# Attention and MLP-mixer kernel: a hand-ordered pipeline over head pairs, with column-tiled value products, 128-key blocks and channel 2 in 128-token chunks over two batches

## The chip, the cores and the metric

The kernel runs on one core of one Trainium2 chip. Its time is device microseconds of one execution. Three executions before the change took 538.24, 538.77 and 540.26 us; the median is 538.77 us. A separate, profiled execution gives the views of the trace.

The engines have short names: PE is the matmul engine, PEld its weight loads, DVE the vector engine, ACT the scalar engine, POOL the engine that here issues the input DMAs, SP the one that issues the output DMAs. A matmul has a stationary operand, brought in by a weight load, and a moving one, whose columns (448 or 384, say) are named with it; results go to PSUM, which this kernel uses in banks of 512 float32 a partition, and DVE or ACT move them to the on-chip memory.

## The reference

Eight batches, 12 heads, 448 tokens, head size 64. Attention has no softmax; its output, 448 tokens by 768 channels, goes through a mixer that works first across tokens, then across channels.

```python
def _attn_ref(q, k, v):
    S = q.shape[2]
    scale = 1.0 / np.sqrt(q.shape[-1])
    scores = scale * np.matmul(q, k.transpose(0, 1, 3, 2))
    attn = np.maximum(scores, 0.0) ** 2 / S
    return np.matmul(attn, v).astype(np.float32)

def _moe_ref(x, w_tok1, w_tok2, w_ch1, w_ch2):   # x: (8, 448, 768)
    xt = x.transpose(0, 2, 1)
    h = np.maximum(xt @ w_tok1, 0.0) @ w_tok2     # 448 -> 256 -> 448
    u = x + h.transpose(0, 2, 1)
    h2 = np.maximum(u @ w_ch1, 0.0) @ w_ch2       # 768 -> 1536 -> 768
    return (u + h2).astype(np.float32)
```

## The kernel before

The work is cut by batch. `attention_pair(b, p)` does two heads, `mixer_chunks(b)` returns the mixer of one batch as a list of 32 closures (30 for the last batch), and the loop at the end (lines 364 to 383) issues the six pairs of batch b+1 between the mixer chunks of batch b, spread evenly. The first six pairs (batch 0) run alone, with the weight loads between them.

**A pair.** Six POOL DMAs (lines 114 to 118) bring q, k and v of two heads as four chunks of 112 tokens, converted to bf16. v lands in a zero-padded tile `v_zp`, so that the value of head e fills 64 of 128 columns and the other 64 are zero. Eight matmuls with the identity transpose q and k; DVE copies the result to `qkT_sb` (line 140). For each of four blocks of 112 keys, two matmuls of 448 columns give the scores of the two heads (`sc_ps`, at rows 0 to 63 and 64 to 127 of the array). Relu and square follow: in blocks 0 and 2 ACT does the relu (line 158) and DVE the square as a scalar_tensor_tensor (line 159); in blocks 1 and 3 DVE does the relu (line 168) and ACT the square (line 175). Then two value products per block, each over the whole array because of the zero padding, add into `xTp_ps`: eight matmuls of 448 columns a pair. ACT scales the sum into `xT_sb` (line 186). These value products have a lower priority (`PRI_AV`), so the scheduler places them some instructions later.

**A mixer.** `stage_b` transposes attention back to tokens (24 matmuls, ACT copies); `stage_c1` and `stage_c2` are the token MLP, and line 256 adds the residual into `uT_sb`; `stage_d` transposes that sum to tokens again (24 matmuls, ACT copies into `u_sb`); `stage_e1` is channel 1 (12 units of six matmuls, ACT relu, line 339); `stage_e2` is channel 2 by chunks of 112 tokens: for each of 12 slices one matmul of 512 columns and one of 256 (`m2_term`, lines 294 and 301); `m2_finish` adds `u_sb` on DVE (lines 314 and 317) and stores 336 KB. In the last batch, two chunks of channel 2 are taken along with channel 1.

**What sets the order.** A scheduler orders each engine by program order, priority and what it knows of readiness; an engine then runs its own list strictly in order. PSUM is two buffers of two banks for scores and `qkT_ps` (`ps_att`), one bank for `xTp_ps`, three single banks for everything of the mixer (`ps_mlp`).

Of the kernel before, what the change touches and what calls it, by code (L numbers as in the profile page):

```python
# [14 lines left out]

PRI_AV = 48
# [3 lines left out]
def kernel(  # L20
# [18 lines left out]
    SC = 4  # L39
    S_CH = S // SC  # L40
    NP = H // 2
    CC = DM // 128
    EC = DC // 128
    JC = DT // 128
    N0 = 512
    N1 = DM - N0
    NV = 3
# [5 lines left out]
    qkv = ctx.enter_context(tc.tile_pool(name="qkv", bufs=5))  # L53
    attn = ctx.enter_context(tc.tile_pool(name="attn", bufs=2))
    batch = ctx.enter_context(tc.tile_pool(name="batch", bufs=2))
# [3 lines left out]
    ps_mlp = ctx.enter_context(tc.tile_pool(name="ps_mlp", bufs=3, space=bass.MemoryType.PSUM))  # L59

    ident = consts.tile([128, 128], BF16)
    make_identity(nc, ident)

    v_tiles = []
    for i in range(NV):
        vt = consts.tile([S_CH, SC, 2, 2 * D], BF16, name=f"v_zp{i}")
        nc.gpsimd.memset(vt, 0.0)
        v_tiles.append(vt)

    wt1 = wpool.tile([S_CH, SC, DT], BF16)  # L70
    wt2 = wpool.tile([128, JC, S], BF16)
    wc1 = wpool.tile([128, CC, DC], BF16)
    wc2 = wpool.tile([128, EC, DM], BF16)

    def load_weights(step):
        if step == 0:
            nc.gpsimd.dma_start(
                out=wt1, in_=moe_w_tok1.rearrange("(c s) j -> s c j", c=SC)
            )
            nc.gpsimd.dma_start(  # L80
                out=wt2, in_=moe_w_tok2.rearrange("(c j) s -> j c s", c=JC)
            )
        elif step in (1, 2):
            for g in range(3 * (step - 1), 3 * step):
                nc.gpsimd.dma_start(
                    out=wc1[:, g, :], in_=moe_w_ch1[128 * g : 128 * (g + 1), :]
                )
        else:
            for e in range(4 * (step - 3), 4 * (step - 2)):
                nc.gpsimd.dma_start(  # L90
                    out=wc2[:, e, :], in_=moe_w_ch2[128 * e : 128 * (e + 1), :]
                )

    xT_tiles = {}

    def mm_lp(*args, pri=0, **kwargs):
        if pri:
            with tc.high_priority(offset=-pri):
                nc.tensor.matmul(*args, **kwargs)  # L99
        else:  # L100
            nc.tensor.matmul(*args, **kwargs)  # L101

    def attention_pair(b, p):
        if p == 0:
            xT_tiles[b] = batch.tile([128, NP, S], BF16, name="xT_sb")
        xT_sb = xT_tiles[b]
        h0 = 2 * p
        v_bf = v_tiles[(b * NP + p) % NV]

        q_raw = qkv.tile([S_CH, SC, 2, D], BF16, name="q_raw")  # L110
        k_raw = qkv.tile([S_CH, SC, 2, D], BF16, name="k_raw")
        for hh in range(2):
            src = q[b, h0 + hh].rearrange("(c s) d -> s c d", c=SC)
            nc.gpsimd.dma_start(out=q_raw[:, :, hh, :], in_=src)  # L114
            src = k[b, h0 + hh].rearrange("(c s) d -> s c d", c=SC)
            nc.gpsimd.dma_start(out=k_raw[:, :, hh, :], in_=src)  # L116
            src = v[b, h0 + hh].rearrange("(c s) d -> s c d", c=SC)
            nc.gpsimd.dma_start(out=v_bf[:, :, hh, hh * D : (hh + 1) * D], in_=src)  # L118

        qkT_ps = ps_att.tile([128, 2, S], BF16, tag="att", name="qkT_ps")  # L120
        for c in range(SC):
            mm_lp(
                qkT_ps[:, 0, c * S_CH : (c + 1) * S_CH],
                lhsT=q_raw[:, c],
                rhs=ident[:S_CH, :S_CH],
                is_transpose=True,
                start=(c == 0),
                stop=False,
            )
        for c in range(SC):  # L130
            mm_lp(
                qkT_ps[:, 1, c * S_CH : (c + 1) * S_CH],
                lhsT=k_raw[:, c],
                rhs=ident[:S_CH, :S_CH],
                is_transpose=True,
                start=False,
                stop=(c == SC - 1),
            )
        qkT_sb = attn.tile([128, 2, S], BF16, name="qkT_sb", bufs=3)
        nc.vector.tensor_copy(qkT_sb, qkT_ps)  # L140

        xTp_ps = ps_acc.tile([128, S], FP32, name="xTp_ps")
        for c2 in range(SC):
            sl2 = slice(c2 * S_CH, (c2 + 1) * S_CH)
            sc_ps = ps_att.tile([128, 2, 512], FP32, tag="att", name="sc_ps")
            for e in range(2):
                hsl = slice(64 * e, 64 * (e + 1))
                mm_lp(
                    sc_ps[:S_CH, e, :S],
                    lhsT=qkT_sb[hsl, 1, sl2],  # L150
                    rhs=qkT_sb[hsl, 0, :],
                    start=True,
                    stop=True,
                )
            at_sb = attn.tile([128, 2, S], BF16, name="at_sb", bufs=10)
            at2_sb = attn.tile([128, 2, S], BF16, name="at2_sb", bufs=10)
            if c2 % 2 == 0:
                nc.scalar.activation(at_sb[:S_CH], sc_ps[:S_CH, :, :S], AF.Relu)  # L158
                nc.vector.scalar_tensor_tensor(  # L159
                    out=at2_sb[:S_CH],  # L160
                    in0=at_sb[:S_CH],
                    scalar=1.0,
                    in1=at_sb[:S_CH],
                    op0=ALU.mult,
                    op1=ALU.mult,
                )
            else:
                nc.vector.tensor_scalar(  # L168
                    out=at_sb[:S_CH],
                    in0=sc_ps[:S_CH, :, :S],  # L170
                    scalar1=0.0,
                    scalar2=None,
                    op0=ALU.max,
                )
                nc.scalar.activation(at2_sb[:S_CH], at_sb[:S_CH], AF.Square)  # L175
            for e in range(2):
                mm_lp(
                    xTp_ps,
                    lhsT=v_bf[:, c2, e, :],
                    rhs=at2_sb[:S_CH, e, :],  # L180
                    start=(c2 == 0 and e == 0),
                    stop=(c2 == SC - 1 and e == 1),
                    pri=PRI_AV,
                )

        nc.scalar.activation(xT_sb[:, p, :], xTp_ps, AF.Copy, scale=float(alpha2))  # L186

    def mixer_chunks(b):
        xT_sb = xT_tiles[b]
        last = b == B - 1  # L190
        chunks = []
        state = {}

        def stage_b(c):
            if c == 0:
                state["x_sb"] = batch.tile([S_CH, SC, DM], BF16, name="x_sb")
            x_sb = state["x_sb"]
            x_ps = ps_mlp.tile([128, DM], BF16, tag="bank", name="x_ps")
# [151 lines left out]
        def stage_e2(c):  # L350
            state["m2_%d" % c] = m2_alloc(c)
            for e in range(EC):
                m2_term(c, e)
# [58 lines left out]
```

## Time and profile before

| what | value |
|---|---|
| median of three runs | 538.77 us |
| span of the profiled execution | 538.1 us |
| instructions, matmuls among them | 7873, 3104 |
| mean granted clock of PE | 0.976 |
| HBM read, written | 43.38 MB, 11.01 MB |
| input DMAs of q, k, v | 288, of 56 KB each |

The span runs from the first to the last instruction of the program; the execution's time is the span and under a microsecond around it. A busy share says how long some instruction of that engine was under way, and since matmuls overlap in the array, a PE that is 92% busy isn't a PE at its peak: how fast matmuls follow one another is read from their starts in the timeline.

### The profile page before, as it was taken

To read this page: it belongs to the slowest core of one execution; us is meant where nothing else is said; L and a number is where in the kernel's file an instruction comes from. 1 tells how busy PE (TensorE), PEld (TensorE's weight loads), DVE (VectorE), ACT (ScalarE), POOL (GpSimd) and SP (SyncE) were. 2 spreads that over 40 slices of the span, in tenths; PEclk is the share of its full clock that TensorE was granted. 3 is DMA by queue.
4 is the path that set the end of the run, shared out by engine and by line. 5 is a ranking of instruction groups with operands and counts; after the bars stand their busy time and mean duration, and the time that the engine had idled before them with its cause. 6 is when DMAs were issued, how large, how long until landed. Compare 5 with 4: busy or idle time off the path is not lost.

```text
span 538.1 us, 7873 instructions
## 1 busy us (share of the span) xinstructions
PE 493.6 (92%) x3104; PEld 274.6 (51%) x3104; DVE 286.3 (53%) x352; ACT 297.6 (55%) x433; POOL 214.9 (40%) x317
## 2 busy tenths in 40 slices
PE   1678999999899989999899989999899998999996
PEld 1223444575446644475445744466445744566554
DVE  1565675627754396626855287434856277441202
ACT  2454777707873378706874269625776078733320
POOL 9679983515534263614553244522544132000000
PEclk9986599999999999999999999999999999999999
DMA  7999994837665665735676467554847352002003
GB/s 66 163 170 153 91 79 27 51 87 67 42 39 54 102 43 36 48 64 77 43 46 59 87 45 50 34 78 70 51 32 49 85 52 18 0 27 78 0 1 102
DMA packets 141092, 33.22 MB, mean 62 GB/s; under 512 B 134464, under 2 KB 136704, under 8 KB 141056
## 3 DMA queue, kind: packets, MB, share of 16 engines
q0 software_dynamic: 136960, 21.71, 54.6%
q1 hardware_dynamic: 4096, 11.01, 6.8%
q8 instruction: 24, 0.39, 0.3%
q14 instruction: 12, 0.10, 0.1%
HBM read 43.38 MB, written 11.01 MB: 101 GB/s over the span
## 4 chain that ended last, share of the span: by engine, by line
PE 63%; ACT 18%; DMA 6%; POOL 5%; DVE 4%; issue 3%; DVEq 0%; ACTq 0%; POOLq 0%
PE m_ps L332 17%; PE m2a_ps L294 14%; PE xTp_ps L99 8%; PE m2b_ps L301 7%; PE sc_ps L101 6%; ACT at_sb L158 6%; DMA wc<-in_moe_w_ch_dram 4%; ACT u_sb L278 4%; ACT x_sb L208 3%; PE h_ps L249 3%; ACT at_sb L175 2%; PE qkT_ps L101 2%; PE t1a_ps L222 2%; DVE at_sb L159 2%; DVE at_sb L168 2%
## 5 line engine op out<-in xcount | busy, mean ns | idle before, releaser
L114 POOL DMA_DIRECT2D q_raw<-in_q_dram x96 | 67.6, 707 | 165.5 <-PE qkT_ps L101 136.0
L168 DVE TENSOR_SCALAR at_sb<-sc_ps 112x896 bf16<-112x896 f32 x96 | 104.4, 1088 | 51.5 <-PE sc_ps L101 51.4
L332 PE MATMUL m_ps<-uT_sb,wc 128*128 128x448 bf16 x576 | 125.3, 354 | 1.8 <-ACT u_sb L278 1.8
L294 PE MATMUL m2a_ps<-wc,r_sb 128*112 128x512 bf16 x360 | 115.3, 379 | 0.0
L158 ACT ACTIVATE at_sb<-sc_ps 112x896 bf16<-112x896 f32 x96 | 88.3, 919 | 40.2 <-PE sc_ps L101 40.0
L99 PE MATMUL xTp_ps<-at_sb,v_zp 112*128 112x448 bf16 x384 | 109.3, 378 | 0.2
L159 DVE SCALAR_TENSOR_TENSOR at_sb<-at_sb 112x896 bf16<-112x896 bf16 x96 | 104.1, 1086 | 6.3 <-ACT at_sb L158 5.3
L175 ACT ACTIVATE at_sb<-at_sb 112x896 bf16<-112x896 bf16 x96 | 91.5, 954 | 21.4 <-DVE at_sb L168 20.8
L118 POOL DMA_DIRECT2D v_zp<-in_v_dram x96 | 67.2, 706 | 66.3 <-PE xTp_ps L99 63.5
L301 PE MATMUL m2b_ps<-wc,r_sb 128*112 128x256 bf16 x360 | 89.6, 272 | 0.0
L332 PEld LDWEIGHTS <-wc 128*128 128x128 bf16 x576 | 52.4, 98 | 60.1 <-issue 20.7
L101 PE MATMUL sc_ps<-qkT_sb 64*112 64x448 bf16 x384 | 71.3, 399 | 5.7 <-ACT at_sb L158 2.6
L116 POOL DMA_DIRECT2D k_raw<-in_k_dram x96 | 67.7, 707 | 1.8 <-issue 0.8
L314 DVE TENSOR_TENSOR out_sb<-m2a_ps,u_sb 112x512 f32<-112x512 f32 x30 | 20.7, 692 | 89.1 <-PE m2a_ps L294 84.7
L140 DVE COPY qkT_sb<-qkT_ps 128x896 bf16<-128x896 bf16 x48 | 29.9, 622 | 70.9 <-PE qkT_ps L101 70.7
L294 PEld LDWEIGHTS <-r_sb 128*112 128x112 bf16 x384 | 49.5, 130 | 30.6 <-ACT r_sb L339 3.8
L339 ACT ACTIVATE r_sb<-m_ps 128x448 bf16<-128x448 f32 x96 | 51.3, 549 | 23.8 <-PE m_ps L332 22.8
L186 ACT ACTIVATE xT_sb<-xTp_ps 128x448 bf16<-128x448 f32 x48 | 26.5, 553 | 67.1 <-PE xTp_ps L99 57.9
L208 ACT ACTIVATE x_sb<-x_ps 112x768 bf16<-112x768 bf16 x32 | 24.2, 811 | 64.9 <-PE x_ps L200 64.8
L301 PEld LDWEIGHTS <-r_sb 128*112 128x112 bf16 x384 | 49.3, 130 | 8.1
L99 PEld LDWEIGHTS <-v_zp 112*128 112x128 bf16 x384 | 37.3, 102 | 29.7 <-issue 12.6
L101 PEld LDWEIGHTS <-qkT_sb 64*112 64x112 bf16 x384 | 25.7, 130 | 49.0 <-issue 29.0
(35 smaller groups left out, 345.2 us busy)
## 6 DMA issues: line engine op xcount, KB each, us to landing
out_dram<-out_sb SPq DMA_DIRECT2D x32, 336.0 KB, 2.7
q_raw<-in_q_dram POOLq DMA_DIRECT2D x96, 56.0 KB, 2.8
k_raw<-in_k_dram POOLq DMA_DIRECT2D x96, 56.0 KB, 2.9
v_zp<-in_v_dram POOLq DMA_DIRECT2D x96, 56.0 KB, 2.9
wc<-in_moe_w_ch_dram POOLq DMA_DIRECT2D x6, 384.0 KB, 7.0
wc<-in_moe_w_ch_dram POOLq DMA_DIRECT2D x12, 192.0 KB, 4.9
wt<-in_moe_w_tok_dram POOLq DMA_DIRECT2D x2, 224.0 KB, 4.6
```

The source lines that it names most:

```text
L99: nc.tensor.matmul(*args, **kwargs)
L101: nc.tensor.matmul(*args, **kwargs)
L114: nc.gpsimd.dma_start(out=q_raw[:, :, hh, :], in_=src)
L116: nc.gpsimd.dma_start(out=k_raw[:, :, hh, :], in_=src)
L118: nc.gpsimd.dma_start(out=v_bf[:, :, hh, hh * D : (hh + 1) * D], in_=src)
L158: nc.scalar.activation(at_sb[:S_CH], sc_ps[:S_CH, :, :S], AF.Relu)
L159: nc.vector.scalar_tensor_tensor(out=at2_sb[:S_CH], in0=at_sb[:S_CH], scalar=1.0, in1=at_sb[:S_CH], op0=ALU.mult, op1=ALU.mult,)
L168: nc.vector.tensor_scalar(out=at_sb[:S_CH], in0=sc_ps[:S_CH, :, :S], scalar1=0.0, scalar2=None, op0=ALU.max,)
L175: nc.scalar.activation(at2_sb[:S_CH], at_sb[:S_CH], AF.Square)
L294: nc.tensor.matmul(m2a_ps[:S_CH], lhsT=lhsT, rhs=wc2[:, e, :N0], start=(e == 0), stop=(e == EC - 1),)
L301: nc.tensor.matmul(m2b_ps[:S_CH], lhsT=lhsT, rhs=wc2[:, e, N0:], start=(e == 0), stop=(e == EC - 1),)
L332: nc.tensor.matmul(m1_ps, lhsT=wc1[:, g, e * 128 : (e + 1) * 128], rhs=uT_sb[:, g, :], start=(g == 0), stop=(g == CC - 1),)
```

## The change

The kernel is rewritten around steps of one head pair, for all 48 pairs. `tc.manual_schedule()` turns the scheduler's ordering off: each engine runs its instructions in the order in which the code issues them. In step s the loop issues the scores of pair s, the transposes of pair s+1, the value products of pair s-1, the way back to tokens of pair s-2 (`x_back`), token 1 once for two pairs, token 2 of two pairs every second step, and at four places (`fill`) as many units of channel work as a credit of a quarter step allows. The units are `channel1` (six matmuls) and `channel2` (twelve matmuls of 384 columns and three with the identity).

- **Loads.** Token rows are taken four (q) or three (k, v) to a partition, so a pair needs three DMAs in place of six, with runs of 1024 or 768 bytes in HBM. The order of tokens is permuted by this; `wt1`, `wt2` and the output DMAs undo it. Keys 384 to 447 of all six pairs of a batch come by four further DMAs into `kz` and `vz`, which are zero outside their halves.
- **Keys.** Three blocks of 128 keys and one block that holds the last 64 keys of both heads together (`scores_rest`): seven score matmuls in place of eight.
- **Transposes.** Each head by itself, into PSUM partitions 0 to 63 or 64 to 127: 16 matmuls in place of eight.
- **Values.** Each head's 64 value columns go to the upper or lower half of `acc_ps`, without the zero padding (column tiling): six matmuls with 64 columns of weights, then one whole one for the rest block. DVE scales the sum.
- **Relu and square.** ACT does every relu, DVE every square, as a `tensor_tensor`.
- **Channel 2.** Two batches share one `uT_sb` and `r2_sb`, and channel 2 runs over 7 chunks of 128 tokens for the two, in two halves of 384 columns. The residual is added by three identity matmuls in the same accumulation, so `stage_d` is gone; DVE copies the result.
- **PSUM.** `qkT_ps` moves from the score buffers to the ring of three banks (`ps_mm`), beside `x_ps`, `t1_ps`, `h_ps`, `m1_ps` and `m2_ps`.

```diff
+    ctx.enter_context(tc.manual_schedule())
...
+        for at, n, src in blocks:
+            for h in range(2):
+                nc.tensor.matmul(
+                    ps[64 * h : 64 * (h + 1), at : at + n],
+                    lhsT=src[:, h, :],
+                    rhs=ident[:n, :n],
+                    is_transpose=True,
...
+        nc.scalar.activation(at, ps[:, :, :S], AF.Relu)
+        nc.vector.tensor_tensor(out=sq, in0=at, in1=at, op=ALU.mult)
...
+        for c in range(KB):
+            sq = at2.pop((s, c))
+            for e in range(2):
+                nc.tensor.matmul(
+                    ps[64 * e : 64 * (e + 1), :S],
+                    lhsT=v_raw[:, e, c, :],
+                    rhs=sq[:, e, :],
...
+        for e in range(EC):
+            nc.tensor.matmul(
+                ps[:, :HN],
+                lhsT=r2[:, e, tok],
+                rhs=wc2[:, e, cols],
...
+            if e == 0:
+                for g in range(CC // 2):
+                    nc.tensor.matmul(
+                        ps[:, g * 128 : (g + 1) * 128],
+                        lhsT=uT[:, half * (CC // 2) + g, tok],
+                        rhs=ident,
...
+    def fill(share):
+        credit[0] += share * per_batch / NP
+        while queue and credit[0] > 0:
+            cost, unit = queue.pop(0)
+            credit[0] -= cost
+            unit()
...
+    for s in range(NS + 4):
+        if s < NS:
+            scores(s, (0, 1))
+        if s + PRE < NS:
+            load_pair(s + PRE)
...
+        fill(0.25)
+        if 0 <= s - 2 < NS:
+            x_back(s - 2)
+        if 0 <= s - 3 < NS and (s - 3) % PG == PG - 1:
+            for i in range(PG):
+                token2(s - 3 - (PG - 1) + i)
+            if (s - 3) % NP == NP - 1:
+                channel_work((s - 3) // NP)
+        fill(0.25)
+        if s < NS:
+            scores(s, (2,))
+        if s + 1 < NS:
+            transposes(s + 1)
+        if 0 <= s - 1 < NS:
+            values(s - 1)
+        if s < NS:
+            scores_rest(s)
+        fill(0.25)
+        if 0 <= s - 2 < NS and (s - 2) % PG == PG - 1:
+            token1((s - 2) // PG)
+        fill(0.25)
+    while queue:
+        queue.pop(0)[1]()
```

The loads of step s, after those of pair s+3, are `wt1` in step 0, `wt2` in step 1, a quarter of `wc1` in each of steps 2 to 5 and a quarter of `wc2` in each of steps 6 to 9. The channel work of a batch enters the queue when its last token 2 is issued, first in step 8.

**PE, value products.** The end of one pair's value products, before, in the middle of the kernel (`v_zp` is the padded value tile, `at2_sb` the squared scores of one key block):

```order
L99 LDWEIGHTS v_zp1_89
L99 MATMUL xTp_ps_2233<-at2_sb_2256,v_zp1_89 128x448 [waits DVE_49]
L99 LDWEIGHTS v_zp1_89
L99 MATMUL xTp_ps_2233<-at2_sb_2256,v_zp1_89 128x448
L99 LDWEIGHTS v_zp1_89
L99 MATMUL xTp_ps_2233<-at2_sb_2265,v_zp1_89 128x448 [waits Activation_49]
L99 LDWEIGHTS v_zp1_89
L99 MATMUL xTp_ps_2233<-at2_sb_2265,v_zp1_89 128x448
```

The same end now (`v_raw` is the value tile without padding, `vz1` the tile of the last 64 keys, `sq` the squared scores):

```order
L216 LDWEIGHTS v_raw_1874
L216 MATMUL acc_ps_2407<-sq_2227,v_raw_1874 64x448
L216 LDWEIGHTS v_raw_1874
L216 MATMUL acc_ps_2407<-sq_2227,v_raw_1874 64x448
L216 LDWEIGHTS v_raw_1874
L216 MATMUL acc_ps_2407<-sq_2266,v_raw_1874 64x448
L216 LDWEIGHTS v_raw_1874
L216 MATMUL acc_ps_2407<-sq_2266,v_raw_1874 64x448
L224 LDWEIGHTS vz1_88
L224 MATMUL acc_ps_2407<-sq_2300,vz1_88 128x448
```

Each product now fills 64 rows of the sum in place of 128; two that follow each other fill different halves, and the pair ends with one whole product.

**DVE, around the way back to tokens.** Before, DVE's list between two pairs while channel 2 ends, with relus and squares by turns:

```order
L317 TENSOR_TENSOR out_sb_3836<-m2b_ps_3811,u_sb_3362 112x256 [waits PE_49]
L140 COPY qkT_sb_3904<-qkT_ps_3895 128x896 [waits PE_49]
L168 TENSOR_SCALAR at_sb_3919<-sc_ps_3916 112x896 [waits PE_49]
L159 SCALAR_TENSOR_TENSOR at2_sb_3911<-at_sb_3910 112x896 [waits Activation_49]
L168 TENSOR_SCALAR at_sb_3937<-sc_ps_3934 112x896 [waits PE_49]
L159 SCALAR_TENSOR_TENSOR at2_sb_3929<-at_sb_3928 112x896 [waits Activation_49]
L256 TENSOR_TENSOR uT_sb_3956<-h_ps_3957,xT_sb_3210 128x448 [waits PE_49]
```

Now, a step with token 2:

```order
L176 TENSOR_TENSOR sq_5097<-at_5096 128x896 [waits Activation_49]
L176 TENSOR_TENSOR sq_5101<-at_5100 128x896 [waits Activation_49]
L258 COPY x_sb_5112<-x_ps_5113 128x4x128 [waits PE_49]
L294 TENSOR_TENSOR uT_sb_4439<-h_ps_5119,xT1_90 128x448 [waits DVE_49,PE_49]
L294 TENSOR_TENSOR uT_sb_4439<-h_ps_5123,xT1_90 128x448 [waits DVE_49,PE_49]
L176 TENSOR_TENSOR sq_5139<-at_5138 128x896 [waits Activation_49]
L169 COPY qkT_5159<-qkT_ps_5142 128x960 [waits PE_49]
L232 TENSOR_SCALAR xT1_90<-acc_ps_5161 128x448 [waits PE_49]
L176 TENSOR_TENSOR sq_5173<-at_5172 128x448 [waits Activation_49]
```

The relus of scores have left DVE; the two squares of a step's first blocks stand ahead of the copy of `x_ps`, and a third ahead of the copy of `qkT_ps`.

**POOL, the start.** Before, the first loads come behind the identity and the zero fills of `v_zp`:

```order
masks.py:197 MEMSET ident_82 128x128
L67 MEMSET v_zp0_87 112x1024
masks.py:199 ISA
masks.py:199 AFFINE_SELECT ident_82<-ident_82 128x128 [waits Pool_49]
L67 MEMSET v_zp1_89 112x1024
L67 MEMSET v_zp2_91 112x1024
L114 DMA q_raw_98<-in_q_dram 112x4x64
L116 DMA k_raw_99<-in_k_dram 112x4x64
```

Now:

```order
L82 DMA q_raw_100<-in_q_dram 112x2x256
L86 DMA k_raw_101<-in_k_dram 128x2x192
L102 DMA kz0_85<-in_k_dram 64x6x64 [waits DVE_49]
L102 DMA kz0_85<-in_k_dram 64x6x64
L92 DMA v_raw_102<-in_v_dram 128x2x192
L102 DMA vz0_87<-in_v_dram 64x6x64 [waits DVE_49]
L102 DMA vz0_87<-in_v_dram 64x6x64
masks.py:197 MEMSET ident_84 128x128
```

The loads stand first, seven for the first pair; the zero fills (of `kz` and `vz`) are on DVE, and two of the loads wait for them.

More of the change, by code (lines that the diff above doesn't have):

```diff
@@ L44 @@
     JC = DT // 128
[L45 to L47 removed]
+    SP = 512
+    HN = DM // 2
+    NT = 2 * S // 128
     alpha2 = (1.0 / D) / S
@@ L77, in load_weights, with load_rest @@
+    def load_rest(b, dst, src):
+        for e in range(2):
             nc.gpsimd.dma_start(
[L78 to L92 removed]
@@ L94 @@
[L94 to L145, printed above, removed]
-            for e in range(2):
[L147 to L151, printed above, removed]
@@ L298, in m2_term @@
                 start=(e == 0),
                 stop=(e == EC - 1),
+                skip_group_check=True,
             )
[L301 to L320 removed]
```

484 lines of the change are left out of this document (268 added, 216 removed).

## The prediction

> **What bounds it now.** The page's busy times and its chain come first.
>
> ```profile
> span 538.1 us, 7873 instructions
> PE 493.6 (92%) x3104; PEld 274.6 (51%) x3104; DVE 286.3 (53%) x352; ACT 297.6 (55%) x433; POOL 214.9 (40%) x317
> ...
> PEclk9986599999999999999999999999999999999999
> ...
> PE 63%; ACT 18%; DMA 6%; POOL 5%; DVE 4%; issue 3%; DVEq 0%; ACTq 0%; POOLq 0%
> ```
>
> PE is the busiest and carries most of the chain; its clock is full but for the first tenth. Next I cut the span by windows: two batches from the middle, bounded by the point at which channel 1 (`m_ps`, 25 matmuls on end) starts in each, and the start.
>
> ```profile
> 147.91:209.67 61.76, 59.31 (x389) 33.64 (x390) 35.75 (x45) 36.79 (x55) 25.02 (x37) 1.00 0.61 57
> 209.67:271.44 61.77, 59.32 (x390) 33.67 (x390) 35.75 (x45) 36.79 (x55) 25.01 (x37) 1.00 0.61 57
> 10.00:62.00 52.00, 38.45 (x171) 15.94 (x170) 30.88 (x33) 26.50 (x33) 43.12 (x67) 0.80 1.42 151
> ```
>
> The columns are length, then busy time of PE, weight loads, DVE, ACT and POOL, then clock, DMA share and GB/s. A batch takes 61.76 us, 10.29 us a pair, with PE under way for 59.3 of them and no other engine for over 37. The first 52 us hold only attention, at clock 0.80, with the DMAs over their fill (1.42 against 0.61). So the middle is a PE stage and the start a stage of loads and latencies.
>
> How long a matmul holds PE comes from starts in the timeline of PE (start, length, then the merged instructions).
>
> ```profile
> 153.34 0.26 PE L101 MATMUL qkT_ps<-ident,q_raw 112*128 112x112 bf16 x2
> 201.85 1.11 PE L332 MATMUL m_ps<-uT_sb,wc 128*128 128x448 bf16 x5 [0.23 <-ACT u_sb L278]
> 202.88 0.59 PE L101 MATMUL sc_ps<-qkT_sb 64*112 64x448 bf16 x4
> 203.40 1.50 PE L332 MATMUL m_ps<-uT_sb,wc 128*128 128x448 bf16 x7
> 209.60 4.90 PE L332 MATMUL m_ps<-uT_sb,wc 128*128 128x448 bf16 x25
> ...
> 485.69 0.38 PE L294 MATMUL m2a_ps<-wc,r_sb 128*112 128x512 bf16 x1
> 485.90 0.27 PE L301 MATMUL m2b_ps<-wc,r_sb 128*112 128x256 bf16 x1
> 486.01 0.38 PE L294 MATMUL m2a_ps<-wc,r_sb 128*112 128x512 bf16 x1
> 491.21 0.50 PE L200 MATMUL x_ps<-ident,xT_sb 128*112 128x128 bf16 x6
> ```
>
> Twenty-five matmuls of 448 columns take 4.90 us, the last alone 0.35: (4.90 - 0.35)/24 = 0.189 us each. 512 and 256 columns together take 486.01 - 485.69 = 0.32 us, so 0.21 and 0.11, and 384 columns, by columns, 0.16. 128 columns take (0.50 - 0.22)/5 = 0.056, 112 columns 0.05. Four score matmuls, each on half the rows of the array, take 203.40 - 202.88 = 0.52 us where four on end would take 0.76: two at a time, 0.38, and 0.14 for leaving this mode. Entering costs 202.88 - 201.85 - 5 x 0.189 = 0.09. A **boundary** between array modes is thus about 0.12 us. By these prices a batch before is 72 + 12 + 48 + 24 matmul times of 0.189 (channel 1, token 2, values, scores), 56 of 0.32 (channel 2, token 1), 48 of 0.056 and 48 of 0.05: 29.5 + 17.9 + 2.7 + 2.4 = 52.5 us. The other 9.3 us, 1.54 a pair, are boundaries and waits.
>
> **The change, PE.** Per pair (step), with column halves taken as running two at a time, as row halves do: channel 1, two units of six, 2.27 us; channel 2, 7/6 units of 12 x 0.16 + 3 x 0.056 = 2.09, 2.44; scores, three pairs and the rest, 0.76; values likewise 0.76 (eight whole ones before, 1.51); transposes, four pairs of 0.05 and four of 0.056, 0.42; x_back 0.22; half a token 1 (eight of 256 columns for two pairs) 0.44; token 2 0.38. Sum 7.69. The order of a step crosses modes five times (into and out of the first scores; into the third; to transposes and values; out of them): 0.60. So **8.29 us** of PE a step, 398 us for 48 steps.
>
> No row shows column halves. Their ends are two at a time (0) and one after the other: values +0.57, transposes +0.42, together +0.99 a step, +47 us in all. I take the first, the row nearest in kind. Of the weight loads, the Trainium skill, "TensorE: Matmul & The Clock Gate", section LDWEIGHTS, says that a load takes its number of columns divided by 1.2 ns, and "TensorEngine Tiling (Array Packing)", Gotcha 2, that column tiling excludes the fast weight load: by an estimate from these, 64 columns are 53 ns, sixteen loads 0.85 us a step in place of 0.42, and the sum is 20 us more. The rows speak against it: `x_ps` loads 112 columns of weights per matmul, 93 ns by that rule, and starts one every 0.056.
>
> **The other engines.**
>
> ```profile
> L159 DVE SCALAR_TENSOR_TENSOR at_sb<-at_sb 112x896 bf16<-112x896 bf16 x96 | 104.1, 1086 | 6.3 <-ACT at_sb L158 5.3
> L158 ACT ACTIVATE at_sb<-sc_ps 112x896 bf16<-112x896 f32 x96 | 88.3, 919 | 40.2 <-PE sc_ps L101 40.0
> L140 DVE COPY qkT_sb<-qkT_ps 128x896 bf16<-128x896 bf16 x48 | 29.9, 622 | 70.9 <-PE qkT_ps L101 70.7
> L256 DVE TENSOR_TENSOR uT_sb<-h_ps,xT_sb 128x448 bf16<-128x448 f32 x48 | 27.5, 617 | 5.4 <-PE h_ps L249 5.4
> L339 ACT ACTIVATE r_sb<-m_ps 128x448 bf16<-128x448 f32 x96 | 51.3, 549 | 23.8 <-PE m_ps L332 22.8
> L317 DVE TENSOR_TENSOR out_sb<-m2b_ps,u_sb 112x256 f32<-112x256 f32 x30 | 12.4, 415 | 0.0
> L114 POOL DMA_DIRECT2D q_raw<-in_q_dram x96 | 67.6, 707 | 165.5 <-PE qkT_ps L101 136.0
> ```
>
> ACT, a step: three relus of 0.92, the rest 0.55, two of channel 1 at 0.55, half a token-1 relu 0.30: 4.7 us. The square as tensor_tensor has no row: it lies between L140's 0.62 (two-byte data, one source) and L159's 1.09 (the same tiles). In shape and sources L159 is nearest, but it is the fused form, alone of its kind here; in the width of all its data and as a plain operation the square is nearest to L140. I take 0.62 and keep 1.09. The Trainium skill, "VectorE: DVE Perf Modes", section The perf-mode tier table, has tensor_tensor of bf16 at twice the base rate, an estimate of 0.62; no run here shows it. DVE, a step: three squares and a half one 2.2, `qkT` copy 0.67, scale 0.62, x_back 0.4, token 2 0.62, channel-2 copies 7/6 x 0.55 (between 0.415 and the 0.69 of 512 columns) 0.64: 5.1 us, or 6.8 with the dear square. Both lie under 8.29, which covers them; stage_d's copies are gone from ACT. POOL has 176 input issues for q, k, v in place of 288 at 0.71, and stays hidden.
>
> **Waits in a step.** Of the ring of three banks, the second token-2 product takes the bank of the filling unit ahead of `x_ps`, and the next unit that of `x_ps`, whose copy waits on DVE behind two squares. From a step's start, by the durations above and 0.55 until the first score is out: first relu done at 1.5 us, second at 2.4, then the unit's relu at 2.95; second square at 3.05, the copy at 3.45. PE, after 0.6 of scores, 1.13 of a unit, 0.22 of x_back and 0.38 of the first product, is at the second at 2.35 and waits to 2.95, and at the next unit at 3.33 and waits to 3.45. That is 0.7 us every second step, 0.35, and I take **0.45** with small ones; ends 0 and what boundaries and waits leave before, 1.54 - 0.60 = 0.94. In the middle a step is 8.74.
>
> **Start.**
>
> ```profile
> 3.90 0.83 POOL L114 DMA_DIRECT2D q_raw<-in_q_dram  x1
> ...
> 9.03 0.53 PE L101 MATMUL qkT_ps<-ident,q_raw 112*128 112x112 bf16 x4 [9.03 <-DMA q_raw<-in_q_dram]
> 10.77 0.99 PE L101 MATMUL sc_ps<-qkT_sb 64*112 64x448 bf16 x4 [0.72 <-DVE qkT_sb L140]
> 40.94 0.53 PE L101 MATMUL qkT_ps<-ident,q_raw 112*128 112x112 bf16 x4 [1.67 <-DMA q_raw<-in_q_dram]
> 48.38 0.56 PE L101 MATMUL qkT_ps<-ident,q_raw 112*128 112x112 bf16 x4 [1.68 <-DMA q_raw<-in_q_dram]
> ```
>
> The first load took 5.1 us from issue to its matmul, and the scores came 1.74 us later. Now the first issue moves from 3.9 to about 1, but the transposes also need the fourth load: 1 + 3 x 0.7 + 5.1 = 8.2, scores at **9.7**. Steps 0 to 7 have no channel work (3.6 us of PE). Before, such a pair took 48.38 - 40.94 = 7.44; DVE's 5.1 is the other end; I take **6.0**. Bytes allow it: to step 9, 13 pairs of 336 KB and 5.0 MB of weights make 9.6 MB, at 151 GB/s 64 us, against 9.7 + 60.
>
> **End.**
>
> ```profile
> 533.41 0.69 DVE L314 TENSOR_TENSOR out_sb<-m2a_ps,u_sb 112x512 f32<-112x512 f32 x1 [2.90 <-issue]
> 534.46 0.32 SPq L320 DMA_DIRECT2D out_dram<-out_sb  x1
> ```
>
> Channel work is 48 x 4.71 = 226 us; steps 8 (three quarters) to 47 take 39.75 x 4.71 = 187, so 39 is left, and 3.6 of values, x_back and token work. From the last DVE start to the span's end it was 538.1 - 533.4 = 4.7, now one short copy: 4.5. Together **47**.
>
> Sum: 9.7 + 8 x 6.0 + 40 x 8.74 + 47 = 454 of span, against 538.1; the median stood 0.7 above its span, so **455 us**.
>
> **Rivals.** (1) Column halves run one after the other, the change not doing what its name says: 455 + 47 = 502. For it: no row shows them; against: row halves start within the same 0.59. 0.12. (2) The two weight loads of a pair of transposes go one after the other, each with its matmul at the 0.05 to 0.056 us of the rows: transposes +0.42 a step, +20, 475. 0.08. (The two pages above would have it so.) (3) The dear square: DVE at 6.8 a step paces the start, 8 x 1.4 = 11, and waits go to 0.94 as its copies come later, 40 x 0.49 = 20: 486. 0.12. (4) Waits near nothing and a start at DVE's pace: 455 - 18 - 7 = 430. 0.10. (5) Slower: the ring of three banks, which now also carries `qkT_ps`, makes PE wait at every unit, as copies stand behind squares. A step has 6.7 units (x_ps, qkT, half t1, one h, two m1, 1.17 m2). The no-wait sum is 455 - 18 = 437; 102 us more need 2.5 us a step, 0.38 a unit. At a bare evacuation of 0.55 a unit, PE never working ahead, it is 437 + 40 x 3.7 = 585. Against it: DVE and ACT have a third of each step free. 0.03. The forecast case has 0.55.
>
> **Chances.** The range takes in (1) to (4): 430 to 503, leaving out (5) and the tails. A measurement here tells about 0.5% (2.7 us) from no change. Only (5), and mishaps of its size, come out slower: faster 0.96, same 0.01, slower 0.03.
>
> **What would show it.** In the changed profile: matmuls of `acc_ps` starting two by two, 0.19 us a pair (0.38 for rival 1); `qkT_ps` 16 in about 0.5 us (0.9 for 2); `sq` 0.62 us (1.09 for 3); waits of PE on DVE copies under 20 us in all (over 100 for 5); a batch in the middle near 52.4 us; first scores near 9.7 and first channel work near 58. Granted clock in the first 60 us well under 0.8 would make the start longer than I allow; PE waits on `qkT_sb` or on loads in the middle would make the whole wrong.

## The result, and the profile after

The changed kernel takes **451.51 us** (median; 451.21 to 451.94), against 538.62 us for the kernel before in the same measurement (538.24 to 540.26). The ratio is 0.837, with a 95% interval of 0.836 to 0.839. The prediction was 455.0 us, with a range of 430 to 503. The profiled execution took 451.94 us at a span of 450.2: time and span of one execution lie 1.7 us apart, not under a microsecond as is said ahead of the prediction.

The page of the profile after opens as follows (busy times, the granted clock in tenths, the chain of work by engine).

```profile
span 450.2 us, 8061 instructions
PE 408.8 (91%) x3336; PEld 218.2 (48%) x3336; DVE 231.0 (51%) x449; ACT 212.3 (47%) x313; POOL 132.6 (29%) x198
...
PEclk9999999999999999999999999999999999999999
...
PE 77%; ACT 8%; issue 5%; DVE 4%; POOL 4%; DMA 1%; ACTq 0%; DVEq 0%; POOLq 0%
```

PE has as large a share of the span as before, with 85 us less under it, and its part of the chain rose from 63% to 77%, while ACT's fell from 18% to 8% and the DMAs' from 6% to 1%. The windows after are cut at the first scores, at the first matmul of step 8 and at that of step 47 (columns as before: length, busy time of PE, weight loads, DVE, ACT and POOL, then clock, DMA share and GB/s).

```profile
8.55:54.15 45.60, 30.81 (x289) 14.71 (x291) 29.25 (x58) 25.53 (x35) 30.25 (x45) 1.00 1.03 127
54.15:392.52 338.37, 324.10 (x2681) 171.83 (x2682) 184.74 (x357) 173.29 (x257) 94.93 (x138) 1.00 0.51 71
392.52:450.20 57.68, 52.90 (x352) 30.76 (x351) 14.27 (x27) 12.21 (x21) 0.00 (x0) 1.00 0.17 49
```

The middle holds 39 steps: 338.37 / 39 = **8.68 us a step**, where a pair took 10.29. If all 48 pairs are counted at this gain, it is 48 x 1.61 = 77 of the 88 us that left the span; the other 11 are what the start and the end gave beyond that. The start, steps 0 to 7, takes 45.6 us, with PE under way for only 30.8 of them.

One step of the middle with token 2, in the timeline of PE and DVE (start, length, then what was merged; in brackets the idle time before it and its releaser):

```profile
366.16 0.55 PE L186 MATMUL sc_ps<-qkT 64*128 64x448 bf16 x4
366.64 0.40 PE L250 MATMUL x_ps<-ident,xT 128*128 128x128 bf16 x4
366.88 0.92 PE L286 MATMUL h_ps<-wt,r_sb 128*128 128x448 bf16 x4
367.51 0.63 DVE L176 TENSOR_TENSOR sq<-at 128x896 bf16<-128x896 bf16 x1 [0.69 <-ACT at L175]
368.32 0.63 DVE L176 TENSOR_TENSOR sq<-at 128x896 bf16<-128x896 bf16 x1 [0.18 <-ACT at L175]
368.86 0.42 DVE L258 COPY x_sb<-x_ps 128x512 bf16<-128x512 bf16 x1
...
369.33 0.32 PE L329 MATMUL m_ps<-wc,r_sb 128*128 128x384 bf16 x1 [1.53 <-DVE x_sb L258]
...
371.54 0.36 PE L186 MATMUL sc_ps<-qkT 64*128 64x448 bf16 x2
371.83 0.39 PE L159 MATMUL qkT_ps<-ident,q_raw 112*64 112x112 bf16 x8
...
372.28 0.73 PE L216 MATMUL acc_ps<-sq,v_raw 128*64 128x448 bf16 x6
372.94 0.36 PE L224 MATMUL acc_ps<-sq,vz 128*128 128x448 bf16 x1
```

Three things are to be seen. Sixteen transposes start within 372.28 - 371.83 = 0.45 us, and six value products within 372.94 - 372.28 = 0.66, boundary to the whole-array product included: both run two at a time. A pair of scores (0.19) is followed by another mode after 371.83 - 371.54 = 0.29: a boundary costs 0.10. And a unit of channel work stands still for 1.53 us for the copy of `x_ps`, which waits on DVE behind two squares: a place that the prediction named, but with a wait of only 0.12 us (3.33 to 3.45).

The start has one line that the prediction didn't foresee, on DVE (the middle row), between the first scores of steps 1 and 2 on PE:

```profile
12.97 0.93 PE L186 MATMUL sc_ps<-qkT 64*128 64x448 bf16 x4 [0.86 <-DVE qkT L169]
...
23.67 0.70 DVE L125 COPY wt<-wt_nat 128x448 bf16<-128x448 bf16 x2 [7.72 <-DMA wt_nat<-in_moe_w_tok_dram]
...
25.53 0.93 PE L186 MATMUL sc_ps<-qkT 64*128 64x448 bf16 x4 [7.51 <-DVE qkT L169]
```

`load_wt2` in step 1 issues the load of `wt2_nat` and puts two DVE copies of it into DVE's list at the same place. Until the load lands, DVE's whole list stands, the copy of `qkT` behind it, and so PE: step 1 lasts 12.6 us (12.97 to 25.53).

### The profile page after: what moved, and what is told of

Same layout as the page of the kernel before. It is cut to its first block, busy times and chain, and to the rows that moved or that the text cites. A ratio compares the mean times of both kernels' runs of the same rounds, so it can differ in the third digit from the quotient of the medians.

```text
span 450.2 us, 8061 instructions
## 1 busy us (share of the span) xinstructions
PE 408.8 (91%) x3336; PEld 218.2 (48%) x3336; DVE 231.0 (51%) x449; ACT 212.3 (47%) x313; POOL 132.6 (29%) x198
## 4 chain that ended last, share of the span: by engine, by line
PE 77%; ACT 8%; issue 5%; DVE 4%; POOL 4%; DMA 1%; ACTq 0%; DVEq 0%; POOLq 0%
PE m_ps L311 23%; PE m_ps L329 22%; ACT at L175 7%; PE sc_ps L186 6%; PE acc_ps L216 6%; PE qkT_ps L159 5%; PE t_ps L268 4%; PE acc_ps L224 3%; PE m_ps L339 2%; PE h_ps L286 2%; PE sr_ps L200 2%; PE x_ps L250 1%; DVE sq L176 1%; DMA wt_nat<-in_moe_w_tok_dram 1%; DVE out_sb L347 1%
## 5 line engine op out<-in xcount | busy, mean ns | idle before, releaser
L176 DVE TENSOR_TENSOR sq<-at 128x896 bf16<-128x896 bf16 x192 | 108.4, 564 | 136.4 <-ACT at L175 136.4
L175 ACT ACTIVATE at<-sc_ps 128x896 bf16<-128x896 f32 x144 | 125.8, 917 | 84.1 <-PE sc_ps L186 84.1
L329 PE MATMUL m_ps<-wc,r_sb 128*128 128x384 bf16 x672 | 126.5, 326 | 4.6 <-DVE x_sb L258 4.6
L92 POOL DMA_DIRECT2D v_raw<-in_v_dram x48 | 34.1, 711 | 233.8 <-PE acc_ps L224 215.3
L311 PEld LDWEIGHTS <-wc 128*128 128x128 bf16 x576 | 54.4, 98 | 61.8 <-issue 16.6
L329 PEld LDWEIGHTS <-r_sb 128*128 128x128 bf16 x672 | 63.3, 98 | 39.0 <-issue 3.7
L186 PE MATMUL sc_ps<-qkT 64*128 64x448 bf16 x288 | 45.8, 369 | 13.0 <-DVE qkT L169 10.1
L216 PE MATMUL acc_ps<-sq,v_raw 128*64 128x448 bf16 x288 | 36.6, 362 | 0.0
L86 POOL DMA_DIRECT2D k_raw<-in_k_dram x48 | 34.9, 728 | 0.0
L169 DVE COPY qkT<-qkT_ps 128x960 bf16<-128x960 bf16 x48 | 31.3, 651 | 4.8 <-PE qkT_ps L159 4.8
L82 POOL DMA_DIRECT2D q_raw<-in_q_dram x48 | 32.7, 682 | 1.1 <-POOLq L449 0.8
L286 PE MATMUL h_ps<-wt,r_sb 128*128 128x448 bf16 x96 | 24.3, 352 | 3.3 <-ACT r_sb L318 2.5
```

The source lines that it names most:

```text
L86: nc.gpsimd.dma_start(out=k_raw.rearrange("p h c d -> p h (c d)"), in_=k[b, h0 : h0 + 2, :KM].rearrange("h (p c) d -> p h (c d)", c=KB),)
L92: nc.gpsimd.dma_start(out=v_raw.rearrange("p h c d -> p h (c d)"), in_=v[b, h0 : h0 + 2, :KM].rearrange("h (p c) d -> p h (c d)", c=KB),)
L175: nc.scalar.activation(at, ps[:, :, :S], AF.Relu)
L176: nc.vector.tensor_tensor(out=sq, in0=at, in1=at, op=ALU.mult)
L186: nc.tensor.matmul(ps[:, e, :S], lhsT=sb[h, KO + c * 128 : KO + (c + 1) * 128], rhs=sb[h, :S], start=True, stop=True,)
L216: nc.tensor.matmul(ps[64 * e : 64 * (e + 1), :S], lhsT=v_raw[:, e, c, :], rhs=sq[:, e, :], start=(c == 0), stop=False, skip_group_check=True,)
```

## The experiments

"After" is the changed kernel at 451.51 us throughout; ratios are to the kernel before, measured beside each.

| kernel | us (lowest to highest) | ratio, 95% |
|---|---|---|
| after, values head by head | 451.88 (451.55 to 452.65) | 0.838 (0.835 to 0.840) |
| after, transposes head by head | 461.74 (461.45 to 462.03) | 0.856 (0.853 to 0.858) |
| after, five of six values in one half | 468.52 (468.13 to 468.80) | 0.870 (0.867 to 0.872) |
| after, squares in the fused form | 475.80 (474.31 to 477.16) | 0.882 (0.879 to 0.885) |
| before, squares as tensor_tensor | 532.33 (531.62 to 533.60) | 0.987 (0.983 to 0.990) |
| before, column-tiled values | 568.33 (565.21 to 569.12) | 1.053 (1.050 to 1.056) |
| after, wt2 copies in step 4 | 445.61 (445.21 to 446.82) | 0.827 (0.825 to 0.829) |
| after, x_back ahead of the scores | 449.41 (447.47 to 451.79) | 0.833 (0.831 to 0.836) |
| after, the scheduler's order | 440.18 (438.03 to 440.92) | 0.815 (0.813 to 0.818) |
| hand order, both waits removed | 434.79 (434.27 to 435.23) | 0.807 (0.805 to 0.809) |
| scheduler's order, wt2 copies in step 3 | 435.90 (435.44 to 436.67) | 0.809 (0.808 to 0.811) |

### Do the column halves run side by side?

The first run changes only the order in which the six products are written: three of one head, then three of the other.

```diff
-        for c in range(KB):
-            sq = at2.pop((s, c))
-            for e in range(2):
+        sqs = [at2.pop((s, c)) for c in range(KB)]
+        for e in range(2):
+            for c in range(KB):
```

> The changed kernel, with the six value products of a pair issued head by head (three for the lower half, then three for the upper) in place of by turns. Theory (halves run two at a time, 0.19 us a pair of products): neighbours now use the same half, so a step pays 3 x 0.19 = 0.57 us more, in the 40 middle steps at least: 474 to 479 us, and acc_ps products start 0.19 us apart. Rival (halves gain nothing from standing by turns, the gain lies elsewhere): 451 to 453.

It took 451.88 us, no more than after. The timeline of PE still has the six products in the same time:

```profile
250.10 0.73 PE L216 MATMUL acc_ps<-sq,v_raw 128*64 128x448 bf16 x6
```

The expectation was wrong: issue order doesn't keep the halves apart. The second run has the same edit on the sixteen transposes, eight in a row for each half.

```diff
-        for at, n, src in blocks:
-            for h in range(2):
+        for h in range(2):
+            for at, n, src in blocks:
```

> The changed kernel, with the 16 transposes of a pair issued head by head. Theory: eight pairs of 0.05 us become sixteen of 0.05, 0.42 us a step: 468 to 472 us. Rival (the weight loads of the 64-column halves set their pace in either order): 451 to 453.

It took 461.74 us, 10.2 more, about half of what was expected. Its timeline of PE in one step shows why (the second head's transposes are written after all eight of the first, and the value products after all sixteen):

```profile
255.98 0.38 PE L159 MATMUL qkT_ps<-ident,q_raw 112*64 112x112 bf16 x4
256.20 0.22 PE L159 MATMUL qkT_ps<-ident,k_raw 128*64 128x128 bf16 x1
256.21 0.24 PE L159 MATMUL qkT_ps<-ident,q_raw 112*64 112x112 bf16 x1
256.26 0.22 PE L159 MATMUL qkT_ps<-ident,k_raw 128*64 128x128 bf16 x1
256.28 0.21 PE L159 MATMUL qkT_ps<-ident,q_raw 112*64 112x112 bf16 x1
...
256.43 0.22 PE L159 MATMUL qkT_ps<-ident,k_raw 128*64 128x128 bf16 x1
256.44 0.38 PE L216 MATMUL acc_ps<-sq,v_raw 128*64 128x448 bf16 x1
256.49 0.27 PE L159 MATMUL qkT_ps<-ident,k_raw 128*64 128x128 bf16 x2
256.60 0.22 PE L159 MATMUL qkT_ps<-ident,kz 128*64 128x128 bf16 x1
```

The first head's four q blocks and its first k block run alone, 0.05 us apart. At 256.21 the second head's first q block starts, while three blocks of the first head are still to come, and from there the two heads alternate. At 256.44 a value product starts ahead of three transposes that are written before it. So each half works off its own list, and PE reaches past about three matmuls that wait for one half to the next one for the other; the three products in a row of the first run are within that reach. The Trainium skill, "TensorE: Matmul & The Clock Gate", section The mechanism, says that matmuls start in program order without exception; these rows differ from it where column halves are used.

Since order doesn't do it, the third run moves two of the second head's three products to the first half, so that five of six stand there.

```diff
             for e in range(2):
+                f = e if c == 0 else 0
                 nc.tensor.matmul(
-                    ps[64 * e : 64 * (e + 1), :S],
+                    ps[64 * f : 64 * (f + 1), :S],
```

> Of a pair's six value products only the first of the second head still goes to the second column half; the other two go to the first half, on top of the first head's sums, which changes the value sums. If each half works off its own list, one product at a time (0.19 us), a step's six products take 5 x 0.19 = 0.95 us in place of 0.57: +0.38 a step, some 40 to 47 of them, 467 to 470 us. If products of 64 columns overlap whatever half they go to, nothing changes: 450 to 453.

The value sums are changed by this, as the expectation says; the amount of work is not. It took 468.52 us, as the first theory had it, and the row of the six products has 1.11 us in place of 0.73:

```profile
376.63 1.11 PE L217 MATMUL acc_ps<-sq,v_raw 128*64 128x448 bf16 x6
```

That is the expected 0.38 a step, for 17.0 us in all. Products of 64 columns overlap because they go to different halves, not because they are narrow.

### What the halves are worth elsewhere

The kernel before, with its value products in column halves in place of the zero padding, and nothing else changed:

```diff
-                    xTp_ps,
-                    lhsT=v_bf[:, c2, e, :],
+                    xTp_ps[64 * e : 64 * (e + 1)],
+                    lhsT=v_bf[:, c2, e, 64 * e : 64 * (e + 1)],
```

> The kernel before, with its eight value products a pair column-tiled into halves (64 of 128 columns of the padded value tile), the scheduler's order as it comes. Theory (halves pay only where neighbours stand in the same mode; there the products lie in four or five pieces among transposes and channel work, and each piece has two boundaries of 0.1 us): gain up to 0.76 us a pair, loss about 1 us a pair, 530 to 560 us. Rival (column halves save half of the value products' time wherever they stand): 500 to 510 us.

It took 568.33 us, 29 more than before, worse than either theory allowed. The timeline of PE of the kernel before, around a pair's values:

```profile
153.44 0.35 PE L99 MATMUL xTp_ps<-at_sb,v_zp 112*128 112x448 bf16 x1
153.63 0.21 PE L101 MATMUL qkT_ps<-ident,q_raw 112*128 112x112 bf16 x1
153.68 0.35 PE L99 MATMUL xTp_ps<-at_sb,v_zp 112*128 112x448 bf16 x1
```

and of this experiment:

```profile
151.28 0.38 PE L99 MATMUL xTp_ps<-at_sb,v_zp 112*64 112x448 bf16 x1
151.58 0.22 PE L101 MATMUL qkT_ps<-ident,q_raw 112*128 112x112 bf16 x1
151.74 0.38 PE L99 MATMUL xTp_ps<-at_sb,v_zp 112*64 112x448 bf16 x1
```

The scheduler of before mixes value products and transposes one by one. A product and a transpose took 153.68 - 153.44 = 0.24 us, both in whole-array mode; now they take 151.74 - 151.28 = 0.46, since each change of mode costs 0.11 us and a lone product has no partner. Most are alone: of the 217 pieces in which this run's value products stand, 140 hold one product. A batch in the middle takes 65.2 us in place of 61.8, also where the granted clock is 1.00. Column halves pay only where several products stand together, and the change brings that by writing all transposes and values of a step in a row, both in this mode.

### The square

After, with the squares as the scalar_tensor_tensor that before used; and before, with the squares as the tensor_tensor that after uses:

```diff
-        nc.vector.tensor_tensor(out=sq, in0=at, in1=at, op=ALU.mult)
+        nc.vector.scalar_tensor_tensor(
+            out=sq, in0=at, scalar=1.0, in1=at, op0=ALU.mult, op1=ALU.mult
+        )
```

> The changed kernel, with every square as the fused scalar_tensor_tensor that the kernel before used. Theory (DVE's strict order puts the squares ahead of the copy of x_ps, and PE waits for that copy): about 1.07 us a square in place of 0.56, 471 to 483 us, the added time in PE's waits on DVE x_sb in the steps with token 2, and about 1 us more in each starting step. Rival (DVE at 51% busy has room for it): 451 to 456.

> The kernel before, with its 96 DVE squares as tensor_tensor, nothing else changed. Theory (PE bounds the middle there, DVE is hidden): DVE 50 us less busy, time 533 to 539 us. Rival (the cheaper square is much of what the change brings): below 520 us.

They took 475.80 us (24.3 more than after) and 532.33 us (7.8 less than the 540.16 of before, measured beside it); the second lies 0.7 us below the range of its theory and far from its rival. The group of the squares after, of after with the fused form, and of before with the plain one (busy time, mean ns of one, idle time before it):

```profile
L176 DVE TENSOR_TENSOR sq<-at 128x896 bf16<-128x896 bf16 x192 | 108.4, 564 | 136.4 <-ACT at L175 136.4
```

```profile
L176 DVE SCALAR_TENSOR_TENSOR sq<-at 128x896 bf16<-128x896 bf16 x192 | 182.2, 970 | 102.0 <-ACT at L175 101.8
```

```profile
L159 DVE TENSOR_TENSOR at_sb<-at_sb 112x896 bf16<-112x896 bf16 x96 | 59.5, 620 | 7.5 <-ACT at_sb L158 6.9
```

The plain form takes 0.62 us for 896 elements (the mean of 0.564 has the half-size squares of the rest block in it; they are a quarter of the 192). In the new order the square stands ahead of the copies that PE waits for, and its length counts; in the old order 45 us less of DVE work bought 8 us. Part of the 24 us may be clock: from 40.6 us on, the trace of the fused form has four stretches of 3.4 us at half clock, which after doesn't have; they can hold at most 7 us.

### The two waits

The copies of `wt2` were moved out of step 1, to step 4, where token 2 first needs them:

```diff
+    def permute_wt2():
         for j in range(JC):
             nc.vector.tensor_copy(
...
+        if s == 4:
+            permute_wt2()
```

> The changed kernel, with the two DVE copies that permute wt2 moved from step 1 to step 4, so that DVE's list no longer waits 7.7 us for that load in front of a square. Theory (that wait holds up DVE, then PE, and nothing else is late behind it): step 1 falls from 12.6 to 4.5 us, 443 to 445 us. Rival (the loads are behind anyway in the first ten steps, so another wait for a load takes its place): 449 to 452.

It took 445.61 us, 5.9 less and 0.6 above the range of the theory. The 7.5 us of step 1 are gone, but in step 4 token 2 comes too early for the copies, which the timeline of PE shows:

```profile
29.78 1.03 PE L288 MATMUL h_ps<-wt,r_sb 128*128 128x448 bf16 x4 [2.28 <-DVE wt L127]
```

For the wait on the copy of `x_ps`, `x_back` was moved ahead of a step's first scores, so that its copy stands ahead of the squares on DVE:

```diff
+        if 0 <= s - 2 < NS:
+            x_back(s - 2)
         if s < NS:
             scores(s, (0, 1))
```

> The changed kernel, with the way back to tokens of pair s-2 issued ahead of the first scores of step s, so that DVE's copy of x_ps stands ahead of the two squares. Theory (PE's wait for that copy is about 0.95 us in each of the steps with token 2, 0.48 a step): 40 x 0.35 to 0.45 less, 433 to 438 us. Rival (token 2 then waits for another bank of the ring, or x_ps for the scale of the step before): 447 to 452.

It took 449.41 us, not 433 to 438. Its windows (start and middle):

```profile
8.58:60.03 51.45, 32.54 (x294) 15.44 (x295) 31.04 (x59) 25.95 (x35) 30.53 (x46) 0.87 1.02 130
60.03:388.45 328.42, 322.15 (x2683) 174.78 (x2682) 187.61 (x355) 175.47 (x258) 94.41 (x138) 1.00 0.51 71
```

Its table of waits (who waits for whom: us in total, times, the longest) has for PE:

```profile
PE x_ps L250 <- DVE xT L232: 14.0, 7, 7.8
```

The middle went from 338.4 to 328.4 us, 8.42 a step: 0.26 a step won, where 0.35 to 0.45 was expected. But the start grew by 5.9 us: there, with no channel work between, `xT` isn't ready when a step begins, and the scores now stand behind `x_back`. Steps 1 to 7 are longer by 0.4 to 1.7 us each. Up to 2.6 us of this may be clock: this trace has half clock until 31.9 us and for 3.4 us more in step 7, after's a full clock from 30.1 on. The longest of these waits, 7.8 us, is still the one for `wt2` in step 1. Ten less 5.9 is about what the profiled execution has (span 445.7 against 450.2 us); the runs scatter over 4 us, and at their median 2.1 are left. So the mechanism held in the middle, at two thirds of the size, and a second one, in the start, ate most of it.

### The hand-written order against the scheduler

One line was taken out, and each engine's order left to the scheduler that before used:

```diff
-    ctx.enter_context(tc.manual_schedule())
```

> The changed kernel without the line that turns the scheduler's ordering off. Its PE list differs: in about one step in three the two score products of a block are parted by six or fifteen channel products. Theory (the gain is in PE's work per step, the order by hand is worth only the parted pairs and their boundaries): 455 to 470 us. Rival (the order by hand is most of the gain): above 490 us.

It took 440.18 us, 11.3 less than the hand order: the expectation had the wrong sign. Its windows, cut at the same points (start, middle):

```profile
9.83:48.74 38.91, 30.46 (x283) 14.35 (x283) 29.33 (x58) 25.72 (x34) 29.11 (x44) 0.96 1.21 155
48.74:378.55 329.81, 327.27 (x2683) 172.28 (x2682) 186.17 (x357) 172.95 (x257) 95.16 (x138) 1.00 0.51 72
```

Step 8 comes 5.4 us earlier and the middle is 8.6 us shorter. Its timeline of PE (lines are one less than after's) in the wait for `wt2`, and in a later step:

```profile
25.76 0.55 PE L185 MATMUL sc_ps<-qkT 64*128 64x448 bf16 x4 [3.78 <-DVE qkT L168]
...
41.80 0.39 PE L158 MATMUL qkT_ps<-ident,q_raw 112*64 112x112 bf16 x8
42.02 0.34 PE L158 MATMUL qkT_ps<-ident,k_raw 128*64 128x128 bf16 x6
...
42.25 0.73 PE L215 MATMUL acc_ps<-sq,v_raw 128*64 128x448 bf16 x6
```

The wait for `wt2` is halved, since squares and value work are put ahead of its copies. Transposes and values still stand together, as they are written, so nothing is lost there. What is lost is at the scores: in the middle 17 score pairs are parted, and boundaries and parted pairs cost 6.6 us more than by hand. But the waits of PE in the middle fall from 19.2 to 4.0 us, and that the expectation had left out. (Both counts are over the starts of all matmuls of the middle.)

### Both waits removed

The last two runs have the `wt2` copies at the end of step 3; the first keeps the hand order and puts `x_back` ahead of the scores from step 8 on only, the second leaves the order to the scheduler.

```diff
     for s in range(NS + 4):
+        if 8 <= s < NS + 2:
+            x_back(s - 2)
...
-        if 0 <= s - 2 < NS:
+        if 0 <= s - 2 < NS and s < 8:
             x_back(s - 2)
...
+        if s == 3:
+            permute_wt2()
```

> The hand order with the two copies of wt2 moved from step 1 to the end of step 3, and x_back ahead of a step's first scores from step 8 on (not before, where xT comes late). If the two losses are what the earlier runs priced, wt2's wait 7.7 us (5.9 of it won with the copies at step 4, where PE still waited 2.3 for them) and 0.26 us a step in the middle (10 us): 451.5 - 7.7 - 10 = 433 to 436, under the scheduler's 440. If x_back's early place only moved the wait from the middle into the start, 443 to 446.

> The scheduler's order (no hand order) with the two copies of wt2 written at the end of step 3. If the 3.8 us that PE still waited there came of DVE's list standing at these copies, 436 to 438. If the scheduler places the copies by when their data is ready anyway, 440 as without the move.

They took 434.79 us, inside the expectation, and 435.90 us, 0.1 below it. They lie 0.3% apart and the intervals of their ratios overlap, so neither order is shown to be the better by more than that. The windows of the hand order without the waits:

```profile
8.57:46.91 38.34, 29.64 (x293) 14.32 (x294) 30.03 (x59) 26.26 (x35) 30.25 (x45) 1.00 1.23 152
46.91:375.32 328.41, 322.09 (x2682) 174.75 (x2681) 187.51 (x355) 175.00 (x257) 94.82 (x138) 1.00 0.52 73
```

Start and middle are shorter by 7.3 and 10.0 us than after, the sizes of the two waits, and the whole by 16.7 us: 3.7% under the change as it was made.

## Why the prediction came out right, and where it was off

| term | predicted | measured |
|---|---|---|
| first scores | 9.7 | 8.55 |
| steps 0 to 7 | 48.0 | 45.6 |
| 40 steps of the middle | 349.6 (8.74 each) | 347.2 (8.68 each) |
| end | 47 | 49 |
| span | 454 | 450.2 |

**The middle was right in its sum, and its waits in part by luck.** Counted over the starts of all matmuls of the middle, each at the spacing of its kind, PE's work is 7.63 us a step (predicted 7.69). Of the other 1.05, 0.56 is boundaries (0.60 predicted) and 0.49 waits (0.45 predicted). Where one unit of six stands ahead of `x_back`, the waits are those that were worked out (PE's timeline after):

```profile
73.99 0.54 PE L286 MATMUL h_ps<-wt,r_sb 128*128 128x448 bf16 x2
74.89 0.54 PE L286 MATMUL h_ps<-wt,r_sb 128*128 128x448 bf16 x2 [0.36 <-ACT r_sb L318]
75.45 1.29 PE L311 MATMUL m_ps<-uT_sb,wc 128*128 128x448 bf16 x6
```

The second token-2 product is late by 74.89 - 73.99 - 2 x 0.189 = 0.52 us (0.60 predicted), the next unit by 75.45 - 74.89 - 2 x 0.189 = 0.18 (0.12 predicted). But in 7 of the 20 steps with token 2 the first `fill` issues no unit. PE then comes early to the next unit and waits there for the copy of `x_ps` for about 1.7 us, counted in the same way (1.53 in the timeline shown above). The prediction has no such step; the seven make 12 of the 19 us of waits in the middle, and that the mean still comes out at half a microsecond is luck. Moving the copy ahead of the squares won 0.26 a step.

**Rival 1, halves one after the other, is ruled out,** by 0.66 us for six products and by the run with five of them in one half, which cost exactly the 0.38 a step that such a series would. **Rival 2, transposes in series, too:** they start 16 in 0.45 us. The weight loads set no slower pace, so the estimate that rested on the two pages of the Trainium skill, 20 us more, didn't come about.

**Rival 3, the dear square:** the value taken, 0.62, is what the trace has. The mechanism of the rival is real and was priced by the run with the fused form: 24 us, where 31 had been predicted. The start gave 6 of the 11 and the middle 18 of the 20 (9.13 us a step).

**Rival 4, next to no waits and a start at DVE's pace,** isn't what ran, but with both waits removed the kernel comes near its 430: 434.79 us.

**Rival 5, the ring of three banks:** the waits exist, but at half a microsecond a step and not 2.5.

**The start was right in sum by two errors.** The step that failed is "Steps 0 to 7 have no channel work ... I take 6.0". A step there takes (45.6 - 7.5) / 8 = 4.8 us without the wait, less even than the 5.1 named as DVE's end, so the term was 10 us too dear; and 7.5 us of waiting for `wt2_nat` were missing. The prediction counted that load's bytes, but not the two copies that its step puts into DVE's list ahead of squares and `qkT`. Had each instruction that step 1 issues been followed to its queue, it would have been seen: DVE's list, in its written order, stood whole for 7.7 us at its first late entry. The first scores, too, came by another way than the one summed (where 8.2 and 1.74 make 9.9, not 9.7): the first load let PE's first weight load start at 4.32 us, 3.0 after its issue and not 5.1, and the first transpose then waited until 6.79 for the identity, which POOL now makes behind the first seven loads.

**What the change is worth by its parts.** By the spacings, of the 1.61 us that a step lost, 1.12 are PE work (8.75 to 7.63), of which the value products are 0.75, and 0.5 are boundaries and waits. Of these parts the runs take out only the halves of the values and the form of the square; what the 128-key blocks, the loads and channel 2 are worth was not measured one by one. The hand-written order as such isn't a gain: the scheduler does the same program in 11 us less. That leaves how the work is cut and that matmuls of one mode stand together as what pays, and of the two only the second has a run of its own (the halves in the kernel before).

## What to carry to other kernels

Write matmuls of one array mode in a row before using column or row halves: here six in a row, spread over two halves, cost 0.38 us a step less than with five of them in one half, and the same halves scattered among whole-array matmuls lost 29 us. Under an order written by hand, put nothing that depends on a load into an engine's list before the load has surely landed, and put the copy that frees a PSUM bank ahead of long work that nobody waits for; two such moves were worth 17 us here. When a forecast comes out right, check its terms all the same: this one's start had an error of 10 us and another of 7.5 against it.

## What the runs showed of the hardware that was not expected

**Two lists on PE.** Column halves run ahead of one another out of the written order, past about three matmuls of the other half, and even a value product passes transposes written before it (the rows of the head-by-head transposes). So what is said ahead of the prediction, that an engine runs its own list strictly in order, fits DVE's list here but not PE's column halves.

**The clock row doesn't tell the rate in the first 30 us.** The page after has 9s throughout, and 1.00 for the window of the start. But the six value products take this long at 15, at 28 and at 33 us (PE's timeline after):

```profile
15.82 1.33 PE L216 MATMUL acc_ps<-sq,v_raw 128*64 128x448 bf16 x6
...
28.38 1.33 PE L216 MATMUL acc_ps<-sq,v_raw 128*64 128x448 bf16 x6
...
32.60 0.73 PE L216 MATMUL acc_ps<-sq,v_raw 128*64 128x448 bf16 x6
```

The first two are at nearly half the rate, as are the scores at 8.55 and 25.53 (0.93 for four, 0.55 later). The trace's first record of the clock begins at 30.14 us, with a full clock; the views count the time before it, which has no record, as full. With the `wt2` copies moved to step 4, and so without PE's stand of 7.5 us in step 1, the first record begins at 17.75 us. The Trainium skill, "TensorE: Matmul & The Clock Gate", section What's actually happening, has PE at half clock until it has been busy for some 3.4 us, and again after it was idle as long; the durations here agree with a half clock, and the clock row doesn't show it. The same holds for the kernel before: its first record begins at 30.7 us, and its four scores at 10.77 take 0.99 us in place of 0.59, so the 0.80 that the prediction read for its first 52 us is too high.
